# A layer norm, attention and feed-forward kernel: four early loads asked for in another order, and one block of products moved ahead of tile 2's transposes

## The chip, the cores and the metric

The kernel runs on one NeuronCore of a Trainium2 chip. The metric is the device time of one execution in microseconds (us). Three timed runs of the kernel before gave 219.34, 219.46 and 219.87 us, median 219.46 us.

## The reference

The input x has 2048 tokens of 640 features in bf16. With xn the layer norm of x, the output is x + s * silu(b):

```python
xn = _layernorm(x, axis=-1)
s = _A_ref(xn, A_wqkv, A_wo)      # linear attention, 32 heads of 20
g = _silu(_B_ref(xn, B_w1, B_w2)) # relu(xn @ w1) @ w2, 1728 hidden features
return x + s * g
```

In _A_ref, q, k and v are xn @ wqkv, phi(t) is t + 1 above zero and exp(t) below, and each head's output is phi(q) (phi(k)^T v) over phi(q) times the sum of phi(k). The result goes through wo.

## The kernel before

All work stands in hand-written order. Every helper appends one operation to the list of one engine (PE, ACT, DVE, POOL, or SP, which only issues DMAs); the lists run in order on each engine, and a small scheduler adds the semaphore waits that the data require. So the order of calls in the source is the order on each engine.

Tokens are cut into 16 tiles of 128 (t) and 4 chunks of 512 (j); features into 5 columns of 128 (k or c); the hidden features into 13 blocks of 128 (f) and a rest of 64. `x_load(t)` (line 337) brings 128 tokens, 160 KB, into `xin`; it lets the caller choose the issuing engine. The weight w1 comes in parts by columns: part 0 is blocks f = 0 to 2, part 1 is f = 3 and 4, part 2 is f = 5 to 8, part 3 the rest. Part 0 is split by rows into two DMAs that ACT issues, `w1_rows` (line 371): the first two feature columns (192 KB), then "the rest", the last three (288 KB). Part 1 (320 KB) and later parts are issued by SP, `w1_load` (line 364).

The change touches the first chunk, tiles 0 to 3, which is handled tile by tile while loads arrive:

- `T_mean` (line 430) is an ACT pass over a tile that sums it for its mean. For tile 0 DVE does part of it (`T_mean0`).
- `center` (line 444) subtracts the mean on DVE and writes `xn`.
- `T_pe` (line 451) transposes the five 128 x 128 columns of a tile on PE against an identity, into one PSUM bank.
- `T_copy` (line 456) brings them from PSUM to `xnT`, on DVE for tiles 0 to 2 (part of tile 0 on ACT), on ACT for tile 3.
- `H_mm` (line 586) multiplies w1's block f with transposed tiles, five matmuls for the five columns. `H_first(t, fs)` (line 628) calls it for one tile and several f, 128 tokens wide. For f = 3 and 4, tiles 0 and 1 are done together, 256 tokens wide (line 668).

In the program the sequence for PE from tile 1 on is: transposes of tile 1, products of tiles 0 and 1 with f = 0 to 2, transposes of tile 2 (line 666), the 256-wide products with f = 3 and 4 of tiles 0 and 1, ten products of tile 2, transposes of tile 3, five and ten more products of tile 2, and 25 products of tile 3. After them come the K projection (`K_mm`, line 474) and the 512-wide blocks of w1 (`H_block`), and so on to the end.

SP's list begins with tile 0, tile 1, tile 2 with a wait for tile 0's landing, w1's part 1, tile 3, then the weight for K (held for the centring of tile 0), w1's part 2 (held for the centring of tile 2), tiles 4 and 5, part 3, tiles 6 and 7, the weight for Q. `extra` in `x_load` and `w_load` is such a wait:

```python
    x0 = x_load(0)
    w1_rows(0, 2, ("w1", 0))
    w1_rows(2, C, ("w1", "rest"))
    x_load(1)
    x_load(2, [x0])
    w1_load(1)
    x_load(3)
```

Of the kernel before, what the change touches and what calls it, by code (L numbers as in the profile page):

```python
# [210 lines left out]
def bass_recurrent_scan__linear_attn_block__dense_activation_relu__prompt_kernel(  # L211
# [14 lines left out]
    P = 128  # L226
# [98 lines left out]
    def dma(E, fn, R=(), W=(), extra=()):  # L325
        last = sc.dsem_last_k
        free = [i for i in range(NDS) if last[i] is None or sc._known(E, ("D", last[i]))]
        i = free[0] if free else min(range(NDS), key=lambda q: last[q])
        return sc.dma(E, fn, i, R=R, W=W, extra=extra)

    def tok(t):
        return slice(P * t, P * (t + 1))
# [4 lines left out]
    def x_load(t, extra=(), E="SP"):  # L337
        sl = t % XR
        return dma(E, lambda eng: eng.dma_start(xin[:, sl, :], x2[tok(t), :]), W=[("xin", sl)], extra=extra)

    def w_load(dst, src, key, extra=(), E="SP"):
        dma(E, lambda eng: eng.dma_start(dst, src.rearrange("(c p) n -> p c n", p=P)), W=[key], extra=extra)
# [21 lines left out]
    def w1_load(i, extra=(), E="SP"):  # L364
        w_load(w1_sb[:, :, W1C[i]:W1C[i + 1]], B_w1[:, W1C[i]:W1C[i + 1]], ("w1", i), extra, E)
# [5 lines left out]
    def w1_rows(c0, c1, key):  # L371
        dma("ACT", lambda eng: eng.dma_start(w1_sb[:, c0:c1, 0:W1C[1]], B_w1[P * c0:P * c1, 0:W1C[1]].rearrange(
            "(c p) n -> p c n", p=P)), W=[key])

    x0 = x_load(0)
    w1_rows(0, 2, ("w1", 0))
    w1_rows(2, C, ("w1", "rest"))
    x_load(1)
    x_load(2, [x0])
    w1_load(1)  # L380
    x_load(3)

# [31 lines left out]
    def xnk(t, cs=range(C)):  # L414
        return [("xn", t, c) for c in cs]
# [14 lines left out]
    def T_mean(t):  # L430
        lo = M0 if t == 0 else 0
        m = 4 if t == 0 else t
        sc.op("ACT", lambda eng: eng.activation(out=ek[:, 0, 0, lo:D], in_=xin[:, t, lo:D], func=ACTF.Copy,
                                                scale=1.0 / D, accum_out=mean[:, m:m + 1]),
              R=[("xin", t)], W=[("mean", m), ("ek_e", 0)])

    def T_mean0():
        sc.op("DVE", lambda eng: eng.tensor_scalar(out=ek[:, 1, 0, 0:M0], in0=xin[:, 0, 0:M0], scalar1=1.0 / D,
                                                   scalar2=0.0, op0=ALU.mult, op1=ALU.add, accum_out=mean[:, 0:1]),
              R=[("xin", 0)], W=[("mean", 0), ("ek_e", 1)])  # L440
# [3 lines left out]
    def center(t, c0, c1):  # L444
        return sc.op("DVE", lambda eng: eng.tensor_scalar(
            out=xn[:, t, P * c0:P * c1], in0=xin[:, t, P * c0:P * c1], scalar1=mean[:, t:t + 1],
            scalar2=mean[:, 4:5] if t == 0 else None, op0=ALU.subtract,
            **(dict(op1=ALU.subtract) if t == 0 else {})),
            R=[("xin", t), ("mean", t)] + [("mean", 4)] * (t == 0), W=xnk(t, range(c0, c1)))

    def T_pe(t, c0, c1, b):
        psb = ps[b].bitcast(bf)
        sc.group("PE", [(lambda eng, c=c: eng.transpose(psb[:, P * c:P * (c + 1)], xn[:, t, P * c:P * (c + 1)], ident[:]))  # L453
                        for c in range(c0, c1)], R=xnk(t, range(c0, c1)) + [("ident",)], W=[("ps", b)])

    def T_copy(E, t, c0, c1, b):
        out = xnT[:, c0:c1, tok(t)]
        src = ps[b].bitcast(bf)[:, P * c0:P * c1].rearrange("p (c q) -> p c q", c=c1 - c0)
        if E == "ACT":
            sc.op("ACT", lambda eng: eng.activation(out=out, in_=src, func=ACTF.Copy), R=[("ps", b)],  # L460
                  W=xtk(t, range(c0, c1)))
        else:
            sc.op("DVE", lambda eng: eng.tensor_copy(out, src), R=[("ps", b)], W=xtk(t, range(c0, c1)))

    def xtk(t, cs=range(C)):
        return [("xnT", t, c) for c in cs]
# [119 lines left out]
    def H_mm(j, f, b, lo=0, hi=512, ks=range(C)):  # L586
        return sc.group("PE", [(lambda eng, k=k: eng.matmul(ps[b][:, lo:hi], lhsT=w1_sb[:, k, P * f:P * (f + 1)],  # L587
                                                            rhs=xnT[:, k, 512 * j + lo:512 * j + hi],
                                                            start=(k == 0), stop=(k == C - 1))) for k in ks],
                        R=w1k(f, ks) + [kk for q in range(lo // P, hi // P) for kk in xtk(4 * j + q, ks)],  # L590
                        W=[("ps", b)])

    def w1k(f, ks):
        i = w1_part(f)
        if i:
            return [("w1", i)]
        return [("w1", 0)] * (min(ks) < 2) + [("w1", "rest")] * (max(ks) >= 2)
# [28 lines left out]
    HF = [2, 3, 4, 5, 6]  # L626
# [7 lines left out]
    fill(8)  # L634
    T_mean0()
    T_mean(0)
    T_mean(1)
    center(0, 0, 2)
    T_pe(0, 0, 2, 7)
# [23 lines left out]
    x_load(6)  # L663
    x_load(7)
    w_load(wqk[:, :, 0:D], A_wqkv[:, 0:D], ("wq",))
    T_pe(2, 0, C, 1)
    T_mean(3)
    for f in (3, 4):
        H_mm(0, f, HF[f], 0, 2 * P)
    T_copy("DVE", 2, 0, C, 1)  # L670
    center(3, 0, C)
    H_first(2, (0, 1))
# [456 lines left out]
```

## Time and profile before

| | us |
|---|---|
| median of three runs | 219.46 |
| the profiled execution | 219.79 |
| its span, first to last instruction | 218.0 |
| PE busy | 214.6 |
| DVE busy | 106.8 |
| ACT busy | 93.1 |

The profiled execution's own time is 1.79 us above its span (what lies around the span) and 0.33 us above the median. Times within the span count from its start. PE is TensorE, PEld its weight loads, ACT ScalarE, DVE VectorE, POOL GpSimd, SP SyncE; ACTq and SPq are the queues of ACT and SP, where a DMA's issue shows. In a timeline, a row is a run of like instructions: start, duration from the first one's start to the last one's end, engine, line, operation, output and input, shape and count; then in brackets the idle time ahead and what ended it. Matmuls overlap in the pipeline, so their rows overlap too, and a short wait of PE shows as a late start of the next row, not as idle time. The line of `H_mm` is 587 (the matmul), of `T_pe` 453, of `T_copy` 463 on DVE and 460 on ACT, of `T_mean` 433, of `center` 445, of `x_load` 339, of `w1_load` 342 and of `w1_rows` 372.

### The profile page before, as it was taken

How to read it: one execution, taken by the hardware profiler on the slowest of the kernel's cores; microseconds unless marked ns; L12 is line 12 of the kernel's file. 1: busy time of each engine (PE TensorE's matmuls, PEld its weight loads, DVE VectorE, ACT ScalarE, POOL GpSimd, SP SyncE). 2: the span in 40 equal slices, each digit the busy share in tenths (PEclk: the TensorE clock that was granted, in tenths of full speed). 3: DMA queues.
4: the chain of work that ended last, by engine and by line, in shares of the span. 5: the costliest groups of instructions: out<-in, count | busy, mean ns of one | idle time of the engine just before them, and what ended most of it. 6: DMA issues, size and time to landing. Idle time of an engine off the chain costs nothing.

```text
span 218.0 us, 3110 instructions
## 1 busy us (share of the span) xinstructions
PE 214.6 (98%) x1224; PEld 109.3 (50%) x1224; DVE 106.8 (49%) x198; ACT 93.1 (43%) x180; POOL 28.5 (13%) x59
## 2 busy tenths in 40 slices
PE   8999999999999999999999999999999999999995
PEld 3975444444444444444464446544444446555574
DVE  3599889894894757666710005711121122230354
ACT  5477558666775669955322213514110211101220
POOL 1065022041110000100000000000000003960001
PEclk9999999999999999999999999999999999999999
DMA  6995578712246424660069988869312313334152
GB/s 189 344 379 99 133 196 199 147 24 51 49 83 120 84 48 81 110 149 0 5 195 360 238 143 225 319 191 347 54 24 44 31 24 65 71 110 152 24 168 90
DMA packets 48507, 29.24 MB, mean 134 GB/s; under 512 B 31508, under 2 KB 47852, under 8 KB 48492
## 3 DMA queue, kind: packets, MB, share of 16 engines
q1 hardware_dynamic: 47820, 28.55, 50.0%
q10 hardware_dynamic: 672, 0.49, 0.7%
q8 instruction: 9, 0.15, 0.3%
q14 instruction: 6, 0.05, 0.1%
HBM read 15.75 MB, written 5.24 MB: 96 GB/s over the span
## 4 chain that ended last, share of the span: by engine, by line
PE 98%; DVE 0%; issue 0%
PE psT L587 26%; PE psT L904 19%; PE psT L572 10%; PE psT L854 8%; PE psT L515 7%; PE psT L947 7%; PE psT L911 7%; PE psT L982 3%; PE psT L478 2%; PE psT L843 2%; PE psT L357 2%; PE psT L617 1%; PE psT L926 1%; PE psT L453 1%; PE psT L863 1%; PE psT L874 1%
## 5 line engine op out<-in xcount | busy, mean ns | idle before, releaser
L587 PE MATMUL psT<-reg 128*128 128x512 bf16 (+2 forms) x325 | 62.5, 338 | 0.0
L904 PE MATMUL psT<-hT,reg 128*128 128x512 bf16 x195 | 44.6, 379 | 0.0
L587 PEld LDWEIGHTS psT<-reg 128*128 128x128 bf16 x325 | 28.8, 99 | 28.1 <-issue 0.4
L600 ACT ACTIVATE hT<-psT 128x512 bf16<-128x512 f32 x52 | 30.6, 598 | 15.9 <-PE psT L587 15.8
L954 DVE TENSOR_TENSOR er<-psT,ek 128x512 bf16<-128x512 f32 x15 | 10.4, 692 | 48.4 <-PE psT L947 48.4
L904 PEld LDWEIGHTS psT<-hT,reg 128*128 128x128 bf16 x195 | 18.9, 98 | 22.3 <-issue 0.7
L942 ACT ACTIVATE ek<-psT 128x512 bf16<-128x512 f32 x15 | 8.3, 598 | 42.3 <-PE psT L929 21.9
L572 PE MATMUL psT<-reg 128*128 128x512 bf16 x100 | 24.8, 379 | 0.0
L962 POOL TENSOR_TENSOR reg<-reg 128x640 bf16<-128x640 bf16 x8 | 10.9, 1390 | 90.8 <-DMA reg<-er 90.8
L515 PE MATMUL psT<-reg 128*128 128x512 bf16 x75 | 18.5, 379 | 0.0
L947 PE MATMUL psT<-pqT,reg 128*128 128x512 bf16 x75 | 18.1, 379 | 0.0
L580 DVE TENSOR_SCALAR er<-psT 128x512 bf16<-128x512 f32 x20 | 13.7, 686 | 8.9 <-ACT er L579 8.9
L854 PE MATMUL psT<-reg 128*128 128x512 bf16 x80 | 17.4, 379 | 0.0
L572 PEld LDWEIGHTS psT<-reg 128*128 128x128 bf16 x100 | 9.8, 98 | 11.8
L911 PE MATMUL psT<-reg,hT 128*128 128x320 bf16 x104 | 15.3, 299 | 0.0
L524 DVE TENSOR_SCALAR ek<-psT 128x512 bf16<-128x512 f32 x15 | 10.1, 676 | 9.4 <-ACT ek L523 9.4
L579 ACT ACTIVATE er<-psT 128x512 bf16<-128x512 f32 x20 | 12.0, 599 | 5.4 <-PE psT L572 5.4
L582 DVE SCALAR_TENSOR_TENSOR pqT<-er 128x512 bf16<-128x512 bf16 x20 | 13.8, 692 | 0.7
L403 DVE BATCH_NORM_STATS2 stats<-reg 128x6 f32<-128x320 bf16 x32 | 13.8, 473 | 0.5 <-DMA reg<-in_A_x_dram 0.5
L866 DVE TENSOR_TENSOR reg<-psT,m 120x120 bf16<-120x120 f32 x6 | 1.7, 283 | 23.3 <-PE psT L863 23.3
L911 PEld LDWEIGHTS psT<-reg,hT 128*128 128x128 bf16 x104 | 10.1, 98 | 4.8 <-issue 0.3
L854 PEld LDWEIGHTS psT<-reg 128*128 128x128 bf16 x80 | 7.8, 98 | 9.3
(77 smaller groups left out, 183.7 us busy)
## 6 DMA issues: line engine op xcount, KB each, us to landing
reg<-in_A_x_dram SPq DMA_DIRECT2D x16, 160.0 KB, 4.2
rscr<-rden SPq DMA_DIRECT2D x4, 640.0 KB, 8.2
reg<-rscr SPq DMA_DIRECT2D x5, 512.0 KB, 6.9
reg<-in_A_x_dram SPq DMA_DIRECT2D x4, 640.0 KB, 7.6
out_dram<-reg SPq DMA_DIRECT2D x15, 160.0 KB, 1.9
reg<-in_A_wqkv_dram SPq DMA_DIRECT2D x2, 800.0 KB, 6.7
reg<-in_B_w_dram SPq DMA_DIRECT2D x1, 1120.0 KB
reg<-in_B_w_dram SPq DMA_DIRECT2D x1, 960.0 KB, 8.3
```

Of the source, the lines that this page charges most:

```text
L403: sc.op("DVE", lambda eng, a=a: eng.bn_stats(stats[:, t, a, :], xv[:, HN * a:HN * (a + 1)]), R=[("xin", t % XR)], W=[("stats", t, a)])
L515: lastK[0] = sc.group("PE", [(lambda eng, k=k: eng.matmul(ps[b], lhsT=wqk[:, k, D + P * m:D + P * (m + 1)], rhs=xnT[:, k, schunk(j)], star ...
L572: sc.group("PE", [(lambda eng, k=k: eng.matmul(ps[b], lhsT=wqk[:, k, P * f:P * (f + 1)], rhs=rhs(k), start=(k == 0), stop=(k == C - 1))) f ...
L579: sc.op("ACT", lambda eng: eng.activation(out=e_, in_=ps[b], func=ACTF.Exp), R=[("ps", b)], W=[("er_e", es)])
L580: sc.op("DVE", lambda eng: eng.tensor_scalar(out=r_, in0=ps[b], scalar1=0.0, scalar2=1e-6, op0=ALU.max, op1=ALU.add), R=[("ps", b), ("er_e ...
L582: sc.op("DVE", lambda eng: eng.scalar_tensor_tensor(out=pqT[:, f, schunk(j)], in0=e_, scalar=1.0, in1=r_, op0=ALU.min, op1=ALU.add), R=[(" ...
L587: return sc.group("PE", [(lambda eng, k=k: eng.matmul(ps[b][:, lo:hi], lhsT=w1_sb[:, k, P * f:P * (f + 1)], rhs=xnT[:, k, 512 * j + lo:512 ...
L600: sc.op("ACT", lambda eng: eng.activation(out=hT[:, f, schunk(j)], in_=ps[b], func=ACTF.Relu), R=[("ps", b)], W=[("hT", j, f)])
L854: ag = sc.group("PE", [(lambda eng, t=t: eng.matmul(ps[b][:, 0:KW], lhsT=xn[:, t, P * k:P * (k + 1)], rhs=pk[:, t, 0:KW], start=(t == 0), ...
L904: sc.group("PE", [(lambda eng, f=f: eng.matmul(ps[b], lhsT=w2_sb[:, f, P * m:P * (m + 1)], rhs=hT[:, f, schunk(j)], start=(f == 0 and not ...
L911: sc.group("PE", [(lambda eng, f=f: eng.matmul(ps[b][:, 0:HN], lhsT=hT[:, f, tok(t)], rhs=w2_sb[:, f, HN * n:HN * (n + 1)], start=(f == 0 ...
L947: sc.group("PE", [(lambda eng, c=c: eng.matmul(ps[b], lhsT=wf[:, c, P * m:P * (m + 1)], rhs=pqT[:, c, schunk(j)], start=(c == 0), stop=(c ...
```

## The change

Three edits. Tile 2's load leaves SP and its wait for tile 0's landing goes; ACT issues it instead, in ACT's list behind `T_mean(0)`, ahead of `T_mean(1)`. With it gone, SP issues w1's part 1 and tile 3 directly behind tile 1. And the 256-wide product with f = 3 of tiles 0 and 1 moves ahead of tile 2's transposes; that with f = 4 stays behind them.

```diff
-    x0 = x_load(0)
+    x_load(0)
     w1_rows(0, 2, ("w1", 0))
     w1_rows(2, C, ("w1", "rest"))
     x_load(1)
-    x_load(2, [x0])
     w1_load(1)
     x_load(3)
...
     T_mean0()
     T_mean(0)
+
+    x_load(2, E="ACT")
     T_mean(1)
...
     w_load(wqk[:, :, 0:D], A_wqkv[:, 0:D], ("wq",))
+    H_mm(0, 3, HF[3], 0, 2 * P)
     T_pe(2, 0, C, 1)
     T_mean(3)
-    for f in (3, 4):
-        H_mm(0, f, HF[f], 0, 2 * P)
+    H_mm(0, 4, HF[4], 0, 2 * P)
     T_copy("DVE", 2, 0, C, 1)
```

PE's order of matmuls around tile 2's transposes, before, from the products of tile 1 (the 21 rows of 128 x 128) on; the line with `ident` is a tile's transposes, `reg` holds w1 and the transposed tiles:

```order
L587 MATMUL psT<-reg 128x128 x21
L453 MATMUL psT<-ident,reg 128x128 x5
L587 MATMUL psT<-reg 128x256 x10
L587 MATMUL psT<-reg 128x128 x10
L453 MATMUL psT<-ident,reg 128x128 x5
L587 MATMUL psT<-reg 128x128 x40
```

And of the change (its lines stand one number lower):

```order
L586 MATMUL psT<-reg 128x128 x21
L586 MATMUL psT<-reg 128x256 x5
L452 MATMUL psT<-ident,reg 128x128 x5
L586 MATMUL psT<-reg 128x256 x5
L586 MATMUL psT<-reg 128x128 x10
L452 MATMUL psT<-ident,reg 128x128 x5
L586 MATMUL psT<-reg 128x128 x40
```

Five of the ten 256-wide matmuls have passed tile 2's transposes; between those transposes and tile 2's first products five are left of ten.

SP's order at the start of the program, before; `in_A_x` is a tile of x, `in_B_w` a part of w1, `in_A_wqkv` the weight for K:

```order
L339 DMA reg<-in_A_x_dram 128x640 x3
L342 DMA reg<-in_B_w_dram 128x5x256
L339 DMA reg<-in_A_x_dram 128x640
L342 DMA reg<-in_A_wqkv_dram 128x5x640
L342 DMA reg<-in_B_w_dram 128x5x512
```

And of the change:

```order
L339 DMA reg<-in_A_x_dram 128x640 x2
L342 DMA reg<-in_B_w_dram 128x5x256
L339 DMA reg<-in_A_x_dram 128x640
L342 DMA reg<-in_A_wqkv_dram 128x5x640
L342 DMA reg<-in_B_w_dram 128x5x512
```

Two tiles instead of three stand ahead of w1's part 1 (the 128x5x256 one). The third is in ACT's order, whose first rows before are these (the 256-wide ACTIVATE is tile 0's sum, the first 640-wide one tile 1's):

```order
L372 DMA reg<-in_B_w_dram 128x2x384
L372 DMA reg<-in_B_w_dram 128x3x384
L433 ACT_TABLE_LOAD
L433 ACTIVATE ek,mean<-reg 128x256
L433 ACTIVATE ek,mean<-reg 128x640
```

And of the change:

```order
L372 DMA reg<-in_B_w_dram 128x2x384
L372 DMA reg<-in_B_w_dram 128x3x384
L432 ACT_TABLE_LOAD
L432 ACTIVATE ek,mean<-reg 128x256
L339 DMA reg<-in_A_x_dram 128x640
L432 ACTIVATE ek,mean<-reg 128x640
```

Tile 2's load has moved from SP's third place to ACT's third DMA, between the sums of tiles 0 and 1.

## The prediction

> **What bounds the kernel now.** I read the page's busy times and the chain that ended last, then PE's timeline of the first 15 us, then the waits of the engines that feed PE there, then the DMA rows.
>
> ```profile
> PE 214.6 (98%) x1224; PEld 109.3 (50%) x1224; DVE 106.8 (49%) x198; ACT 93.1 (43%) x180; POOL 28.5 (13%) x59
> PE 98%; DVE 0%; issue 0%
> ```
>
> PE is busy nearly always and is the whole chain. So the time changes by what PE waits, and the change touches only the first 13 us. Busy time hides waits shorter than a matmul's pipeline, so I take starts from PE's timeline:
>
> ```profile
> 5.10 1.01 PE L587 MATMUL psT<-reg 128*128 128x128 bf16 x9
> 5.95 0.44 PE L453 MATMUL psT<-ident,reg 128*128 128x128 bf16 x5
> 6.23 1.39 PE L587 MATMUL psT<-reg 128*128 128x128 bf16 x21
> 7.46 0.44 PE L453 MATMUL psT<-ident,reg 128*128 128x128 bf16 x5
> 7.84 1.82 PE L587 MATMUL psT<-reg 128*128 128x256 bf16 x20
> ...
> 9.60 0.45 PE L453 MATMUL psT<-ident,reg 128*128 128x128 bf16 x5
> 9.89 2.53 PE L587 MATMUL psT<-reg 128*128 128x128 bf16 x40
> 12.26 2.88 PE L478 MATMUL psT<-reg 128*128 128x320 bf16 x20
> 14.97 1.24 PE L587 MATMUL psT<-reg 128*128 128x512 bf16 x5
> ...
> 7.84 1.26 PE L587 MATMUL psT<-reg 128*128 128x256 bf16 x10
> ...
> L587 PE MATMUL psT<-reg 128*128 128x256 bf16 x10 | 1.3, 274 | 0.0
> ```
>
> The five transposes from 5.95 to 6.23 go at 0.056 us each: the free pace of a 128-wide matmul. The ten 256-wide ones take 1.26 us with one's own 0.274, so (1.26 - 0.27)/9 = 0.11 each. Counting on from each row, PE should start at 6.23 + 21 x 0.056 = 7.41 (it starts at 7.46), 7.46 + 0.28 = 7.74 (7.84), 7.84 + 10 x 0.11 + 10 x 0.056 = 9.50 (9.60), and 9.89 + 40 x 0.056 = 12.13 (12.26). That is 0.05 + 0.10 + 0.10 + 0.13 = **0.38 us of waits**, all that an order of loads and blocks could remove between 6 and 12.3 us. What ends each stands on ACT and DVE:
>
> ```profile
> 5.65 0.74 ACT L433 ACTIVATE ek<-reg 128x640 bf16<-128x640 bf16 x1
> 6.73 0.38 DVE L445 TENSOR_SCALAR reg<-reg,mean 128x640 bf16<-128x640 bf16 x1
> 7.93 0.49 DVE L463 COPY reg<-psT 128x640 bf16<-128x640 bf16 x1 [0.83 <-PE psT L453]
> 8.29 0.74 ACT L433 ACTIVATE ek<-reg 128x640 bf16<-128x640 bf16 x1 [1.82 <-DMA reg<-in_A_x_dram]
> 9.16 0.39 DVE L445 TENSOR_SCALAR reg<-reg,mean 128x640 bf16<-128x640 bf16 x1 [0.73 <-ACT ek L433]
> 10.09 0.70 ACT L460 ACTIVATE reg<-psT 128x640 bf16<-128x640 bf16 x1 [0.97 <-PE psT L453]
> ```
>
> The wait at 9.60 is tile 3: ACT sums it at 8.29, as it lands, DVE centres it until 9.55, and PE starts 0.05 later. The wait ahead of 12.26 lies inside the 40: after 15 of them (10.73) PE needs ACT's copy, which ends at 10.79. The wait at 7.84 is w1's part 1, by the rows of its load:
>
> ```profile
> 0.78 0.97 ACTq L372 DMA_DIRECT2D reg<-in_B_w_dram  x2
> 0.79 0.88 SPq L339 DMA_DIRECT2D reg<-in_A_x_dram  x2
> 3.23 0.33 SPq L339 DMA_DIRECT2D reg<-in_A_x_dram  x1
> 3.56 0.19 ACT L433 ACTIVATION_READ_ACCUMULATOR ek<-reg 128x1 f32 x1
> 3.60 0.43 SPq L342 DMA_DIRECT2D reg<-in_B_w_dram  x1
> 4.08 0.52 SPq L339 DMA_DIRECT2D reg<-in_A_x_dram  x1
> 4.26 0.74 ACT L433 ACTIVATE ek<-reg 128x640 bf16<-128x640 bf16 x1 [0.52 <-DMA reg<-in_A_x_dram]
> 7.14 0.38 SPq L342 DMA_DIRECT2D reg<-in_B_w_dram  x1
> ...
> reg<-in_B_w_dram ACTq DMA_DIRECT2D x1, 288.0 KB, 3.9
> reg<-in_A_x_dram SPq DMA_DIRECT2D x1, 160.0 KB, 2.3
> reg<-in_B_w_dram SPq DMA_DIRECT2D x1, 320.0 KB, 4.2
> reg<-in_B_w_dram SPq DMA_DIRECT2D x1, 640.0 KB, 5.9
> ```
>
> The last figure of a load's row is the time from issue to landing. Part 1 (320 KB) is asked for at 3.60 and lands at 7.8; tile 2 (160 KB, 2.3) goes from 3.23 to 5.55; w1's rest (288 KB, 3.9), ACT's second issue at about 1.26, lands at 5.16; part 2 (640 KB) goes from 7.14 to 13.0.
>
> **The change part by part.** *Part 1 and tile 3 earlier.* SP is free behind tile 1 at 0.79 + 0.88 = 1.67, so part 1 is asked for at about 1.7 instead of 3.60 and tile 3 at 2.2 instead of 4.08. How full the DMA engines are:
>
> ```profile
> 2.40:4.40 2.00, 2.00 (x7) 0.53 (x5) 1.05 (x4) 1.31 (x4) 0.00 (x0) 1.00 1.08 365
> 4.40:5.00 0.60, 0.60 (x5) 0.28 (x5) 0.40 (x3) 0.60 (x2) 0.00 (x0) 1.00 1.09 341
> 5.00:5.40 0.40, 0.40 (x5) 0.30 (x5) 0.40 (x3) 0.35 (x2) 0.00 (x0) 1.00 0.77 95
> 5.40:5.80 0.40, 0.40 (x6) 0.40 (x5) 0.11 (x1) 0.28 (x2) 0.00 (x0) 1.00 0.66 175
> 5.80:6.40 0.60, 0.60 (x14) 0.60 (x12) 0.14 (x1) 0.60 (x2) 0.00 (x0) 1.00 1.03 300
> ```
>
> The last three columns are PE's granted clock, the share of the 16 DMA engines and GB/s. The engines are full to 5.0 and have a hole until 5.8, where part 1 starts up. Asked for sooner, part 1 fills the hole: 320 KB (328 kB) take 0.9 us at 365 GB/s, 1.1 us at the 300 that it reaches itself from 5.8 on; I take 1.1. It lands at about 6.2 to 6.7, tile 3 at about 6.7 to 7.1, before 7.46 in either order. So the 0.10 wait at 7.84 goes, and so does tile 3's 0.10 at 9.60. Tile 3's sum also no longer follows its landing but tile 2's sum.
>
> *Tile 2 on ACT.* Its issue stands behind the read-out of tile 0's sum (3.56 to 3.75) and ahead of tile 1's sum at 4.26. An ACT issue takes 0.97/2 = 0.49, so it fits the 0.5 us in which ACT was idle for tile 1. If it starts only at 3.75 and runs long, like SP's 0.52, tile 1's sum starts at 4.3 and not 4.26: 0.04 us, with tile 1's transposes at 5.95 some 0.4 us behind its centring. I cost it at nothing; without that cover each 0.1 us would cost the same on PE. The landing is what counts. Alone it would be 3.25 to 3.75 + 2.3 = 5.55 to 6.05; with all of part 1 ahead on the DMA engines, 5.55 + 1.1 = 6.65. I take 6.4, the middle of 6.05 and 6.65.
>
> *Does that do for PE?* From tile 3's row, the sum's start to PE's transposes is 9.60 - 8.29 = 1.31 us. PE now does the f = 3 product first, 7.46 + 5 x 0.11 = 8.01, and reaches tile 2's transposes 0.55 us later than before. So tile 2's sum may start up to 8.01 - 1.31 = 6.70, and 6.4 to 6.65 is in time, the upper end just so.
>
> *The new wait.* Behind the transposes only one 256-wide block is left to hide tile 2's copy. Before, the copy began 0.47 us behind the transposes' start (7.46 to 7.93), took 0.49, and PE starts some 0.06 us behind a releaser: 8.01 + 0.47 + 0.49 + 0.06 = 9.03. PE is through with the transposes and the f = 4 block at 8.01 + 0.28 + 0.55 = 8.84. It **waits 0.19 us**, where two blocks covered the copy. Then ten products of tile 2 take it to 9.03 + 0.56 = 9.59; DVE has centred tile 3 by then (8.97 + 0.39 = 9.36 behind the copy). The 0.13 wait for ACT's copy of tile 3 hangs on PE's own transposes and stays.
>
> *Held loads.* Part 2 of w1 is held for tile 2's centring, which moves from 6.73 to about 7.6; part 2 goes from 7.14 to about 8.0 and with 5.9 us lands at 13.9. Its first reader is the 512-wide block at 14.97, so 1.0 us is left. Tiles 4 to 7 behind it shift by at most that 0.9; DVE's statistics read them off PE's chain.
>
> *Sum.* PE stands at tile 3's transposes at 9.59 instead of 9.60: -0.10 - 0.10 + 0.19 = **-0.01 us**. Everything behind is PE's own pace. The profiled execution's 219.79 becomes 219.78; the median of the runs was 0.33 lower, so I predict **219.45 us**.
>
> **The rivals.** *A: w1's rest comes late.* Part 1 now stands in the other queue beside w1's rest, and both use the same DMA engines. The rest is read at about 5.7 (behind six of the nine matmuls from 5.10: 5.10 + 6 x 0.1), so it has 0.5 us over its landing at 5.16. How two queues share, by DMA packets per queue in the stretches 2.6 to 3.2 and 3.2 to 3.7:
>
> ```profile
> q10 hardware_dynamic: 221, 0.17, 82.2%
> q1 hardware_dynamic: 48, 0.04, 21.8%
> ...
> q1 hardware_dynamic: 127, 0.15, 83.3%
> q10 hardware_dynamic: 67, 0.04, 25.8%
> ```
>
> q10 is ACT's queue, q1 SP's. Whole loads take turns: first w1's first rows, then tile 1, both in the order asked for. That speaks for the rest going ahead of part 1 as a whole, and against A. If they share evenly, up to 288 KB of part 1 go in between: 0.8 us, the rest lands at 5.96, PE stands 0.3 us at 5.7, 219.75. If all 1.1 us go ahead, 0.6 to 0.7 us, 220.1. Decides: a landing after 5.65. The Trainium skill, "DMA: Bandwidth & Descriptors", section "Queues, rings and completion order", says that each DMA engine changes between queues only after a packet of typically 9 to 17 descriptors. By that rule w1's rest, 24 rows per engine, would be broken once; the trace's 221 against 48 shows turns, but no case of a load over 16 rows with a competitor. So A keeps a chance; the estimate by the page is one packet, 0.3 to 0.4 us, still inside the 0.5, and the sum stays.
>
> *B: tile 2 comes too late (slower).* Were loads served in the order asked for through both queues, tile 2 (3.3 to 3.75) stands behind part 1 and tile 3: 5.55 + 1.1 + 0.45 (160 KB at 365 GB/s) = 7.1. Its sum starts 0.4 after the 6.70 allowed, PE idles 0.45 us at L453, the 0.19 behind it stays: 219.9. If K's 800 KB (asked for at 4.6) gets ahead in part too, up to 2.2 us more; a quarter of it makes 220.4. For it: the turns above agree with order of asking as well. Against: so far each queue got its turn.
>
> *C: PE's pace.* One 128-wide matmul lasts 0.44 - 4 x 0.056 = 0.22 us, so the nine of 5.10 go at (1.01 - 0.22)/8 = 0.10 us, the next at 0.056: PE's pace nearly doubles at about 5.8, though the granted clock reads 1.00 on both sides. If that came later, behind the 26 that now end at 7.46, these would take 0.10 instead of 0.058: +1.1, 220.6. If it came before 5.1, -0.4 to -0.6, and with the other waits gone 218.8. Three runs within 0.53 us speak against a swing of 1.1. The Trainium skill's "TensorE: Matmul & The Clock Gate", Part 1, has the pace doubled after a busy window of about 3.4 us that runs freely; by it the point differs from run to run, whatever the kernel. The rows show one such point and no second; the sum stays.
>
> *D: the gain without the new wait*, were the copy hidden after all: -0.20 us, 219.25; at most all 0.38.
>
> **How the numbers follow.** 0.3% is 0.66 us, about what a measurement of this kernel can tell from no change. Forecast 0.42, all within. A 0.15: half within, half slower. B 0.28: 0.15 within, 0.13 slower. C 0.11: 0.05 slower, 0.05 faster, the rest within. D 0.04, within. Together: faster 0.05, same 0.70, slower 0.25. The range 218.9 to 220.6 takes in D, A and most of B, and leaves out the ends of C and of B.
>
> **What would show it.** In the changed profile: five 256-wide matmuls from about 7.46 without a late start; transposes of tile 2 at about 8.0; a late start of tile 2's first products of 0.2 us behind DVE's copy; tile 3's transposes near 9.59; K's matmuls near 12.25. A shows as a gap at 5.7, B as transposes of tile 2 after 8.1 with ACT's third sum after 6.7, C as 128-wide matmuls at 0.1 us after 6. The forecast is wrong if tile 3's transposes stand more than 0.2 us off 9.59.

## The result, and the profile after

Seven runs of the change gave 220.21 to 220.67 us, median 220.27; seven of the kernel before 219.34 to 220.15, median 219.46. The ratio is 1.0035, with a 95% interval of 1.0021 to 1.0049: the change is slower by a third of a per cent. The forecast was 219.45 us, no change. The measured time lies in the stated range, but a small, clear slowdown stands where none was forecast.

The page of the profiled execution of the change, which took 220.67 us:

```profile
span 218.9 us, 3090 instructions
PE 213.2 (97%) x1204; PEld 108.6 (50%) x1224; DVE 106.6 (49%) x198; ACT 92.9 (42%) x180; POOL 28.5 (13%) x59
```

PE's busy time is lower, but 20 of its 1224 matmul records are missing (x1204 against 1224 weight loads), so the two busy times can't be compared; starts can. PE's timeline:

```profile
5.80 0.45 PE L452 MATMUL psT<-ident,reg 128*128 128x128 bf16 x5
6.09 1.94 PE L586 MATMUL psT<-reg 128*128 128x128 bf16 x26
8.30 0.45 PE L452 MATMUL psT<-ident,reg 128*128 128x128 bf16 x5 [0.27 <-DVE reg L444]
8.59 1.48 PE L586 MATMUL psT<-reg 128*128 128x256 bf16 x15
9.91 0.44 PE L452 MATMUL psT<-ident,reg 128*128 128x128 bf16 x5
10.19 2.53 PE L586 MATMUL psT<-reg 128*128 128x128 bf16 x40
12.55 2.88 PE L477 MATMUL psT<-reg 128*128 128x320 bf16 x20
15.48 1.03 PE L586 MATMUL psT<-reg 128*128 128x512 bf16 x4
16.92 1.53 PE L477 MATMUL psT<-reg 128*128 128x320 bf16 x10 [0.41 <-DVE ek L493]
```

The row at 6.09 holds the 21 products of tile 1 and the moved block of five (26 in all). Two rows now show open idle time. Tile 2's transposes start at 8.30, behind DVE's centring; and the third group of the K projection starts at 16.92, behind a DVE step (`K_relu`). From the first K group to the third the kernel before took 16.05 - 12.26 = 3.79 us, here it is 4.37: 0.58 us more. Its row before:

```profile
16.05 1.52 PE L478 MATMUL psT<-reg 128*128 128x320 bf16 x10
```

So this execution loses 12.55 - 12.26 = 0.29 us up to K and 0.58 us behind it, 0.87 together, and the spans differ by 0.9. What stands behind the first is on ACT and DVE (the last row is a load's, with its size and its time from issue to landing):

```profile
3.34 0.35 ACTq L339 DMA_DIRECT2D reg<-in_A_x_dram  x1
...
6.99 0.74 ACT L432 ACTIVATE ek<-reg 128x640 bf16<-128x640 bf16 x1 [1.40 <-DMA reg<-in_A_x_dram]
7.85 0.74 ACT L432 ACTIVATE ek<-reg 128x640 bf16<-128x640 bf16 x1
...
7.85 0.39 DVE L444 TENSOR_SCALAR reg<-reg,mean 128x640 bf16<-128x640 bf16 x1 [1.18 <-ACT ek L432]
8.79 0.49 DVE L462 COPY reg<-psT 128x640 bf16<-128x640 bf16 x1 [0.55 <-PE psT L452]
...
reg<-in_A_x_dram ACTq DMA_DIRECT2D x1, 160.0 KB, 3.6
```

ACT asked for tile 2 at 3.34, as early as SP did before (3.23), but it took 3.6 us to land and not 2.3. The sum of tile 2 (the row at 6.99) waited 1.40 us for it. Tile 3, the row at 7.85, was there already. The copy ends at 9.28. PE is through with the f = 4 block at 8.59 + 0.55 = 9.14 and starts tile 2's ten products at 9.91 - 0.56 = 9.35: a wait of 0.21 us, where the forecast had its new wait of 0.19.

The other loss starts at tile 4, the statistics of which DVE takes ahead of `K_relu`:

```profile
14.99 0.89 DVE L402 BATCH_NORM_STATS2 stats<-reg 128x6 f32<-128x320 bf16 x2 [1.40 <-DMA reg<-in_A_x_dram]
16.03 0.83 DVE L493 TENSOR_SCALAR ek<-psT,rsy 128x640 bf16<-128x640 f32 x1
```

DVE stood 1.40 us for tile 4, its `K_relu` ran from 16.03 to 16.86, and PE started 0.06 later.

### The profile page after: what moved, and what is told of

Its sections match the earlier page's. It is cut to its first block, busy times and chain, and to the rows that moved or that the text cites. A ratio compares the mean times of both kernels' runs of the same rounds, so it can differ in the third digit from the quotient of the medians.

```text
span 218.9 us, 3090 instructions
## 1 busy us (share of the span) xinstructions
PE 213.2 (97%) x1204; PEld 108.6 (50%) x1224; DVE 106.6 (49%) x198; ACT 92.9 (42%) x180; POOL 28.5 (13%) x59
## 4 chain that ended last, share of the span: by engine, by line
PE 91%; DMA 6%; DVE 1%; issue 1%; SPq 0%; ACT 0%; ACTq 0%
PE psT L586 23%; PE psT L905 19%; PE psT L571 10%; PE psT L855 8%; PE psT L514 7%; PE psT L948 7%; PE psT L912 7%; DMA reg<-in_A_x_dram 6%; PE psT L983 2%; PE psT L844 2%; PE psT L477 1%; PE psT L616 1%; PE psT L927 1%; PE psT L864 1%; PE psT L875 1%
## 5 line engine op out<-in xcount | busy, mean ns | idle before, releaser
L586 PE MATMUL psT<-reg 128*128 128x512 bf16 (+2 forms) x318 | 61.0, 336 | 0.6 <-issue 0.2
L586 PEld LDWEIGHTS psT<-reg 128*128 128x128 bf16 x325 | 28.3, 98 | 28.2 <-DVE reg L462 0.5
L571 PE MATMUL psT<-reg 128*128 128x512 bf16 x100 | 24.8, 379 | 0.0
L514 PE MATMUL psT<-reg 128*128 128x512 bf16 x72 | 17.8, 379 | 0.2
L948 PE MATMUL psT<-pqT,reg 128*128 128x512 bf16 x71 | 17.3, 379 | 0.2
L855 PE MATMUL psT<-reg 128*128 128x512 bf16 x78 | 17.3, 379 | 0.1
L571 PEld LDWEIGHTS psT<-reg 128*128 128x128 bf16 x100 | 9.8, 98 | 11.8
L855 PEld LDWEIGHTS psT<-reg 128*128 128x128 bf16 x80 | 7.8, 98 | 9.3
```

Source lines behind the costliest of these rows:

```text
L514: lastK[0] = sc.group("PE", [(lambda eng, k=k: eng.matmul(ps[b], lhsT=wqk[:, k, D + P * m:D + P * (m + 1)], rhs=xnT[:, k, schunk(j)], star ...
L571: sc.group("PE", [(lambda eng, k=k: eng.matmul(ps[b], lhsT=wqk[:, k, P * f:P * (f + 1)], rhs=rhs(k), start=(k == 0), stop=(k == C - 1))) f ...
L855: ag = sc.group("PE", [(lambda eng, t=t: eng.matmul(ps[b][:, 0:KW], lhsT=xn[:, t, P * k:P * (k + 1)], rhs=pk[:, t, 0:KW], start=(t == 0), ...
L948: sc.group("PE", [(lambda eng, c=c: eng.matmul(ps[b], lhsT=wf[:, c, P * m:P * (m + 1)], rhs=pqT[:, c, schunk(j)], start=(c == 0), stop=(c ...
```

## The experiments

Theories at the start. H: the larger part, 0.58 us, comes from w1's part 2 and tile 4 being asked for later, since they are held for tile 2's centring. R: tile 2's late landing alone makes the loss. On the landing itself, S: loads asked for ahead of tile 2 delay it. All ratios are to runs of the kernel before measured beside the version, with 95% intervals. The starts, in us, come from one profiled execution each; "K wait" is the distance of the first and third K groups less 3.79. In brackets stands the kernel that a version was made from, where the name does not say it:

| kernel | tile 2's sum | tile 2's transposes | tile 3's | first K group | K wait | ratio |
|---|---|---|---|---|---|---|
| before | 5.65 | 7.46 | 9.60 | 12.26 | 0 | |
| before, again | 5.82 | 7.50 | 9.43 | 12.08 | 1.17 | |
| the change | 6.99 | 8.30 | 9.91 | 12.55 | 0.58 | 1.0035 (1.0021 to 1.0049) |
| the change, again | 7.06 | 8.37 | 9.97 | 12.62 | 0 | |
| hold on tile 1 (change) | 7.08 | 8.38 | 9.99 | 12.64 | 0 | 1.0025 (1.0014 to 1.0036) |
| hold later (before) | 5.64 | 7.20 | 9.13 | 11.77 | 0.01 | 0.9996 (0.9983 to 1.0010) |
| loads alone | 7.21 | 8.51 | 10.45 | 13.10 | 0 | 1.0043 (1.0028 to 1.0058) |
| block alone | 5.66 | 8.09 | 9.69 | 12.33 | 0.01 | 0.9996 (0.9980 to 1.0013) |
| tile 3 on ACT (change) | 6.61 | 8.41 | 10.01 | 12.65 | 0.01 | 1.0016 (1.0007 to 1.0025) |
| tile 2 third on ACT (change) | 6.91 | 8.39 | 9.99 | 12.63 | 0.84 | 1.0014 (0.9997 to 1.0032) |
| part 1 waits (change) | 7.69 | 9.00 | 10.61 | 13.25 | 0.01 | 1.0038 (1.0025 to 1.0051) |
| tile 2 without wait (before) | 5.85 | 7.31 | 9.24 | 11.88 | 0.01 | 1.0005 (0.9991 to 1.0020) |
| part 2 early (before) | 6.11 | 7.41 | 9.35 | 12.00 | 0 | 1.0018 (1.0002 to 1.0035) |

In eleven of the thirteen profiles the span is the first K group's start plus the K wait plus 205.7 us, within 0.1; in the other two (before, again, and tile 2 third on ACT) it is 0.3 to 0.4 us more. So nearly all that separates the profiled executions is read from these two columns.

**The hold moved to tile 1.** In the change:

```diff
-    center(1, 0, C)
+    held1 = center(1, 0, C)
...
-    w1_load(2, [held])
+    w1_load(2, [held1])
```

> The change, with w1's part 2 (and so tiles 4 to 7 behind it on SP) held for the centring of tile 1 instead of tile 2. Theory H (0.58 of the change's 0.87 us on PE comes from part 2 and tile 4 being asked for late: tile 4 lands at 14.96, DVE's K_relu for tile 0 ends late, PE waits for it at K's third group at 16.92): part 2 is asked for at about 5.8, tile 4 lands before 13.5, the wait ahead of K's third group goes, that group starts at 16.35 +- 0.1, the time is 0.3 us above before (219.7 to 219.8). Rival R (tile 2's late landing alone drives it, part 2's asking has no part): the time stays at 220.2 to 220.3.

Measured: 220.27 us median of 11 runs, 1.0025. Part 2 was asked for at 5.70, tile 4 landed at 12.3, there was no K wait, and the third group started at 16.43, as H said for the trace. The time did not follow as far: the median is 0.57 us above that of the runs of before beside it (219.70), where H had 0.3 and the change stands at 0.81. The intervals of the two ratios overlap, so a small share of the hold is neither shown nor excluded. But the profiled execution, without a K wait, still took 220.17 us. PE's rows tell why:

```profile
7.08 0.74 ACT L432 ACTIVATE ek<-reg 128x640 bf16<-128x640 bf16 x1 [1.55 <-DMA reg<-in_A_x_dram]
...
8.38 0.45 PE L452 MATMUL psT<-ident,reg 128*128 128x128 bf16 x5 [0.43 <-DVE reg L444]
8.67 1.48 PE L586 MATMUL psT<-reg 128*128 128x256 bf16 x15
9.99 0.44 PE L452 MATMUL psT<-ident,reg 128*128 128x128 bf16 x5
```

Tile 2's transposes wait for tile 2 just the same. Most of the loss is there without a K wait.

**The hold made later in the kernel before**, its counterpart (`T_copy` also returns its operation now, so that a load can wait for it):

```diff
-    held = center(2, 0, C)
+    center(2, 0, C)
...
+    T_pe(2, 0, C, 1)
+    T_mean(3)
+    for f in (3, 4):
+        H_mm(0, f, HF[f], 0, 2 * P)
+    held = T_copy("DVE", 2, 0, C, 1)
     w1_load(2, [held])
...
-    T_pe(2, 0, C, 1)
-    T_mean(3)
-    for f in (3, 4):
-        H_mm(0, f, HF[f], 0, 2 * P)
-    T_copy("DVE", 2, 0, C, 1)
```

> The kernel before, all its loads of tiles 0 to 3 and w1's part 1 as they were, with part 2 and what stands behind it on SP held for DVE's copy of tile 2 instead of its centring: asked for at about 8.45 instead of 7.14. Theory H: tile 4 lands at 14.7 to 15.0, PE waits 0.5 to 0.7 us ahead of K's third group with tile 2 as punctual as before; 220.0 to 220.1. Rival R: no change, 219.4 to 219.6.

Measured: 219.53 us, 0.9996; part 2 was asked for at 8.20, 1.1 us later than before, and tile 4 still landed at about 13.4. H falls: asking 1.1 us later costs nothing, and asking 2.6 us sooner, in the version above, gained less than H said. The same profile shows what PE does when tile 2 is punctual:

```profile
5.97 1.39 PE L587 MATMUL psT<-reg 128*128 128x128 bf16 x21
7.20 0.44 PE L453 MATMUL psT<-ident,reg 128*128 128x128 bf16 x5
7.48 1.81 PE L587 MATMUL psT<-reg 128*128 128x256 bf16 x20
9.13 0.44 PE L453 MATMUL psT<-ident,reg 128*128 128x128 bf16 x5
11.77 2.88 PE L478 MATMUL psT<-reg 128*128 128x320 bf16 x20
```

The products behind the transposes start 0.28 us behind them, and tile 3's transposes at 7.48 + 1.10 + 0.56 = 9.14: neither of the two waits of 0.10 that the first profile of before had. Against the kernel with the hold on tile 1 it is 12.64 - 11.77 = 0.87 us up to K. This execution is the quickest of its twelve (219.32 us), so 0.87 is an upper figure for what separates the medians of the change and of before (0.81).

**Both kernels profiled a second time**, unchanged.

> The kernel before, unchanged, looked at a second time. If its first profile (219.79 us, above the median) was a late one of its kind: part 1 lands before 7.5, PE's transposes of tile 2 start at 7.2 and of tile 3 at 9.1 to 9.2, waits of 0.2 us and not 0.38 from 6 to 12.3, first K group at 11.8 to 11.9. If it was typical: 7.46, 9.60, 12.26 again.

> The change, unchanged, looked at a second time. If the wait ahead of K's third group (16.92 in its first profile, behind tile 4's landing at 14.96) belongs to that execution alone: tile 4 lands before 14, no wait there, tile 2 lands at 6.9 to 7.1, PE waits 0.5 to 0.6 us at its transposes and 0.2 at its copy, first K group at 12.5 to 12.7. If it belongs to the change: tile 4 at 14.9 and the wait again.

The second execution of before, 221.1 us, has the largest K wait of all, 1.17 us; in it tile 4 took 7.5 us to land, from 7.61 to 15.1:

```profile
17.04 1.53 PE L478 MATMUL psT<-reg 128*128 128x320 bf16 x10 [1.01 <-DVE ek L494]
...
reg<-in_A_x_dram SPq DMA_DIRECT2D x1, 160.0 KB, 7.5
```

Its part 1 landed at 7.3, and its waits of 0.10 are gone (7.50 + 0.28 = 7.78), as the first alternative had it; but PE was slower than that to its transposes, 7.50 and 9.43. The second execution of the change, 220.15 us, has no K wait; tile 4, asked for 1.1 us later than in before's second execution, took 4.4 us and landed at 13.2, 2 us sooner. So the K wait comes and goes with the execution in either kernel. Tile 2 landed at 7.0, as expected, but PE did not wait 0.5 us for it:

```profile
6.64 1.88 PE L586 MATMUL psT<-reg 128*128 128x128 bf16 x26
8.37 0.45 PE L452 MATMUL psT<-ident,reg 128*128 128x128 bf16 x5
```

At PE's own pace 6.64 + 21 x 0.056 + 5 x 0.11 = 8.37, the very start of the transposes. PE was late here by itself: its 128-wide products went at 0.107 us each up to 6.6 and only then at 0.056 (tile 1's transposes, from 6.15 to 6.64, took 0.49 us and not 0.28). Tile 2's centring was done just in time for it. In the change's first execution the same sum gives 6.09 + 1.18 + 0.55 = 7.82, and the wait is 0.48 us.

**The change's parts by themselves.** The loads without the moved block, and the block without the loads (each is the diff of the change without the other part).

> The change without the moved block: tile 2 on ACT, part 1 and tile 3 early, f = 3 and 4 both behind tile 2's transposes as before. Tile 2's transposes wait for its centring at 8.30 in either order, so 0.55 us more work lies behind them and tile 3's transposes come at about 10.25 instead of 9.91. Theory H: K's third group is still set by tile 4's landing (16.9), so the total stays that of the change, 220.2 to 220.3: the two waits do not add, the later one decides. Rival (waits add up on PE): 220.6.

> The kernel before with the moved block alone (f = 3 ahead of tile 2's transposes), all loads as before. Theory L (the change's loss is tile 2's late landing plus the cover taken from tile 2's copy): tile 2 is punctual, so the transposes start without a wait for its centring, but PE waits 0.20 to 0.21 us for tile 2's copy, and at the f = 3 block 0 to 0.5 us for part 1, which lands at 7.25 to 7.8; 219.7 to 220.1. Rival (the moved block costs nothing when tile 2 is punctual): 219.4 to 219.6.

The loads alone cost the most: 220.61 us, 1.0043. PE stands idle 0.98 us for tile 2's centring:

```profile
8.51 0.45 PE L452 MATMUL psT<-ident,reg 128*128 128x128 bf16 x5 [0.98 <-DVE reg L444]
8.80 1.81 PE L586 MATMUL psT<-reg 128*128 128x256 bf16 x20
10.45 0.44 PE L452 MATMUL psT<-ident,reg 128*128 128x128 bf16 x5
```

Here H's expectation (the total stays) failed and the rival's 220.6 came out: nothing behind hides the later transposes. The block alone is not told from before (219.77 us, 0.9996). Its profile has the copy's wait as expected (8.37 + 0.55 = 8.92, and ten products end where tile 3's transposes start, 9.69 - 0.56 = 9.13: 0.21 us), no wait for part 1, and ends up 0.25 us behind before's second execution at the first K group. The interval of the ratio reaches to 1.0013, or 0.29 us, so the runs neither show nor exclude the cost of 0.2 us in time.

**What delays tile 2.** Tile 3 moved behind tile 2, both issued by ACT:

```diff
     w1_load(1)
-    x_load(3)
...
     x_load(2, E="ACT")
+    x_load(3, E="ACT")
```

> The change with tile 3 asked for by ACT directly behind tile 2 (about 3.7) instead of by SP at 2.18; part 1 still early. Theory S (tile 2's late landing at 6.9 to 7.1 comes from the loads asked for ahead of it, tile 3's share 0.45 us and part 1's share the rest): tile 2 lands at 6.4 to 6.6, PE's transposes of tile 2 start at 7.8 to 7.9 with no wait or under 0.1, only the copy's 0.2 stays; first K group at 12.0 to 12.2; 219.8 to 219.9. Rival U (ACT's issue behind tile 0's sum is itself slow to start, whatever stands ahead): tile 2 lands at 6.9 again, transposes at 8.3, 220.2.

Tile 2 was asked for at 3.44 and took 3.1 us; its sum started at 6.61, 0.4 us sooner than in the change, as S said. PE came to the transposes at 8.41 without waiting for it:

```profile
6.61 0.74 ACT L431 ACTIVATE ek<-reg 128x640 bf16<-128x640 bf16 x1 [0.88 <-DMA reg<-in_A_x_dram]
...
6.64 1.94 PE L585 MATMUL psT<-reg 128*128 128x128 bf16 x26
8.41 0.44 PE L451 MATMUL psT<-ident,reg 128*128 128x128 bf16 x5
```

It came that late by its own pace in this execution (6.64 + 21 x 0.056 + 5 x 0.11 = 8.37). The median is 219.95 us, 1.0016: by the medians, about half of the loss went with tile 3's place. What is left of the delay, 3.1 us against the 2.3 of before, goes with part 1: from 4.8 to 5.4 us, with tile 2 asked for and tile 3 not on SP's queue, the queues moved

```profile
q1 hardware_dynamic: 389, 0.20, 109.0%
q10 hardware_dynamic: 14, 0.01, 5.3%
```

q1 is SP's queue with part 1, q10 ACT's with tile 2.

Then part 1 was put back too, asked for only when tile 0 has landed:

```diff
-    x_load(0)
+    x0 = x_load(0)
...
-    w1_load(1)
     x_load(3)
+    w1_load(1, [x0])
```

> The change with tile 3 early on SP (1.7) and part 1 asked for only when tile 0 has landed (3.3), as ACT asks for tile 2. Theory S: with part 1 no longer ahead tile 2 lands at 5.9 to 6.2, part 1 at 7.3 to 7.6; PE waits 0 to 0.4 us for part 1 at the f = 3 block, then not for tile 2; the copy's 0.2 stays; first K group at 12.0 to 12.4; 219.7 to 220.0. Rival U: tile 2 lands at 6.9 all the same, transposes at 8.3, 220.2.

Both expectations missed. SP asked for part 1 at 3.46, ACT for tile 2 at 3.47, so part 1 was ahead after all, by hundredths; tile 2 took 4.1 us and its sum waited until 7.69. The packets of the two queues between 5.2 and 5.8 us, and the rows that waited:

```profile
q1 hardware_dynamic: 159, 0.08, 56.8%
q10 hardware_dynamic: 37, 0.05, 21.2%
...
7.69 0.74 ACT L432 ACTIVATE ek<-reg 128x640 bf16<-128x640 bf16 x1 [1.94 <-DMA reg<-in_A_x_dram]
8.16 0.72 PE L586 MATMUL psT<-reg 128*128 128x256 bf16 x5 [0.32 <-DMA reg<-in_B_w_dram]
9.00 0.45 PE L452 MATMUL psT<-ident,reg 128*128 128x128 bf16 x5
```

Asked for together, the two loads run mixed, at 78% of the DMA engines' time, and both are late: part 1's block waits at 8.16 too. Tile 3, asked for at 1.7, landed at 5.6, ahead of both, so this run does not single out part 1's share. It shows that two loads asked for at the same time delay each other, which neither expectation had.

Tile 2 as ACT's third DMA:

```diff
     w1_rows(2, C, ("w1", "rest"))
+    x_load(2, E="ACT")
...
-    x_load(2, E="ACT")
```

> The change with tile 2's load as ACT's third DMA directly behind w1's rows, so asked for at about 1.75: after part 1 (1.71), ahead of tile 3 (2.18). ACT's table load and so tile 0's sum come 0.2 us later for it. Theory O (loads are served in the order asked for, whichever queue): tile 2 lands 0.4 to 0.5 us ahead of tile 3, at about 6.5; PE reaches tile 2's transposes at about 8.0 and does not wait, only the copy's 0.2 stays; 219.8 to 219.9. Rival Q (ACT's queue is served only while SP's is empty): tile 2 lands behind tile 3 at about 6.9 as in the change, PE waits 0.3 us at the transposes and 0.2 for the copy; 220.2.

Tile 2 was asked for at 1.78, 1.6 us sooner than in the change, and landed at 6.8, 0.1 us sooner. The order of landing is O's (part 1 at 6.6, tile 2 at 6.8, tile 3 at 7.0), the size is neither's: part 1, which landed at 6.0 in the change, is itself 0.6 us later. The median, 220.17 us, is what Q said; the ratio of 1.0014 is to runs of before with a median of 219.87, and its interval takes in no change. So the time decides nothing here.

**Two versions for a gain.** Tile 2 on SP without its wait, and part 2 held for tile 1 in the kernel before:

```diff
-    x_load(2, [x0])
+    x_load(2)
```

> The kernel before with one edit: tile 2, third on SP, no longer waits for tile 0's landing; part 1 and tile 3 follow at 2.1 and 2.6. Theory O (the DMA engines serve loads in the order asked for, over both queues): w1's rest keeps its landing near 5.2, tile 2 lands at 5.4 to 5.7, part 1 at 6.5, tile 3 at 7.0; the waits at 7.84 and 9.60 go, tile 2's copy stays covered by two blocks; 0.15 to 0.25 us faster than before, 219.2 to 219.3. Rival P (queues take turns in pieces smaller than a load): w1's rest lands after 5.65, PE stands at 5.7, 219.5 to 219.8.

```diff
-    center(1, 0, C)
+    held1 = center(1, 0, C)
...
-    w1_load(2, [held])
+    w1_load(2, [held1])
```

> The kernel before with w1's part 2, and so tiles 4 to 7 behind it, held for the centring of tile 1 instead of tile 2: asked for at 5.7 instead of 7.1. In some profiles of either kernel tile 4 landed at 14.9 to 15.3 and PE waited 0.6 to 1.2 us ahead of K's third group. Theory V (that wait is what spreads the times): tile 4 lands before 13 always, no such wait, first K group at 11.8 to 12.1; median 0.1 to 0.3 us under before, 219.3 to 219.5, and few runs above 219.9. Rival (the spread is of the start, before 12 us): median as before and the same spread.

The first is as fast as before (1.0005); the 0.15 to 0.25 us that O said did not come. Tile 3's transposes follow at 9.24 without the 0.10 waits, but three other executions with before's loads have none either, so there was little to win; w1's rest landed at 5.4, and PE was not held by it. The second is no gain (1.0018, runs from 219.38 to 221.12), and six of its twelve runs are above 219.9 where V had few: V's forecast falls. Its profile, without a K wait, is of a quick run (219.53), so whether its longer runs have one was not seen. What spreads the runs stays open. No version beat the kernel before.

## Why the prediction was wrong

*Tile 2 on ACT: the step that failed.* I put its landing at 6.4, the middle of 6.05 and 6.65, and the latest useful start of its sum at 6.70. It landed at 6.9 and 7.0, and the sum started at 6.99 and 7.06. The limit was right: 1.31 us behind the sum's start PE transposes (8.30 - 6.99). The upper bound of 6.65 was not: it put all of part 1 ahead of tile 2 and left out tile 3, which SP was to ask for at 2.2, over 1 us ahead of tile 2 as well. With tile 3 back behind tile 2 the sum started at 6.61. Tile 3's transposes came at 9.91, 0.32 off the 9.59, which by the forecast's own sign makes it wrong. Rival B had both loads ahead, and its landing at 7.1 was nearly exact; I gave it 0.28 since "each queue got its turn". The rows that I read as turns can be read as order of asking, and the change showed the latter: from 5.2 to 5.8 us, tile 2 asked for long since, the queues moved

```profile
q1 hardware_dynamic: 301, 0.22, 109.2%
q10 hardware_dynamic: 6, 0.01, 3.4%
```

that is, part 1 and tile 3 on SP's queue, and all but none of tile 2. The hole in the DMA engines' work was filled as forecast (357 and 384 GB/s from 5.0 to 5.4 and to 5.8, where before had 95 and 175), but tile 2 paid for it. The Trainium skill, "DMA: Bandwidth & Descriptors", section "Queues, rings and completion order", has each engine alternate between queues at packets. By that alone, tile 2 would have broken into part 1 here. It did so where both were asked for together, and not here, 1.6 us behind part 1; so the rule alone did not forecast this landing. Whether tile 2's packets were ready by then is not shown. The section "Issuing engines are not separate DMA queues" of the same page of the Trainium skill says that issuing from another engine saves issue time alone. The trace agrees: ACT issued the load as early as SP had before (3.34 against 3.23), and the transfer came later.

*The gain of 0.20 us.* It was read from one execution. In it part 1 landed at 7.8 and tile 3 at 8.2; in three others with these loads as before (before again, hold later, part 2 early) part 1 landed at 7.3 to 7.4 and tile 3 by 7.9, and the waits at 7.84 and 9.60 did not exist. The sum should have been 0 + 0.2 for the copy + the wait for tile 2.

*The new wait.* Right: 0.19 forecast, 0.20 to 0.21 in every profile with the moved block, by PE's starts. The runs of the block alone do not show it in time.

*Held loads.* Part 2 was asked for at 8.27, near the forecast 8.0. "DVE's statistics read them off PE's chain" was wrong: tile 4 stands on PE's chain through `K_relu`, and PE waited 0.58 us in the first profile. But it waits so in an execution of before too (1.17 us), and making the hold later there cost nothing.

*The sum*, then: PE reaches tile 2's transposes at 7.20 and 7.41 in two quick executions with before's loads (hold later, part 2 early), and at 8.30 and 8.38 in the change's first execution and with the hold on tile 1. Of the 0.9 to 1.2 us between them 0.55 is the block moved ahead, which is work that PE does in either order. So 0.3 to 0.6 is waiting, and the copy's wait adds 0.2: together 0.5 to 0.8, against the 0.81 between the medians. The two executions profiled first hide this: before's was 0.33 us above its median, and the change's had the K wait.

*Rival A* did not come: w1's rest landed at 5.3 with part 1 asked for behind it. *Rival C*, PE's pace, came in another form. The rows show one such point in each execution, but not at the same place: PE's products reach their shorter spacing between 3.3 and 6.6 us, at 5.8 in the first execution of before. In the change's second execution the point came so late that PE would have reached tile 2's transposes at 8.37 without any wait for tile 2. There the late landing cost nothing; in the change's first execution and with the hold on tile 1 it cost 0.5 and 0.6 us. So the price of the landing is what it adds to PE's own pace, and it differs from run to run. How much of the spread of like runs comes from this (219.21 to 221.12 for the runs of before beside the experiments) is not shown. Nothing shows that the pace differs between the kernels; the loss goes with the loads (the loads alone 1.0043, the block alone 0.9996). The Trainium skill, "TensorE: Matmul & The Clock Gate", Part 1, gives a freely running window for such a point; a shift from one execution to the next, 3.3 to 6.6 us here, agrees.

## What to carry to other kernels

Ask first for the load that is needed first. In these runs giving it to another engine's queue did not let it pass loads that had been asked for over a microsecond before it, and the loads taken "early" for free stood ahead of it. A profile of one execution may hold waits that the next doesn't; where a sum is of tenths of a microsecond, profile the same kernel two or three times before a wait is booked as a gain. Work moved ahead of a wait no longer covers what stands behind it: here the copy's wait was 0.2 us for the 0.55 us moved.

## What the runs showed of the hardware

ACT's issue of a DMA did not wait for the ACTIVATE ahead of it to end, nor for its read-out: the ACTIVATE started at 3.33 and lasted 0.42 us, the issue started at 3.34. Two loads asked for within 0.02 us on different queues ran mixed and took 4.1 and 4.7 us (tile 2 and part 1), where in the five executions with before's loads, part 1 asked for 0.4 us behind tile 2 on one queue, they took 2.2 to 2.6 and 3.5 to 4.2. Tile 4's time from issue to landing was 6.3 and 4.4 us in two executions of the change, 5.9 and 7.5 in two of the kernel before. Why is open; the runs show it in both kernels, and no experiment set it apart.
